# Two evictions of a gated attention and state-space kernel, written in another order of elements

## The chip, the core and the metric

The kernel runs on one core of one Trainium2 chip. The metric is the device time of one execution in microseconds. Before the change the median of three runs is 440.37 us (440.08 to 440.7). Busy times, waits and durations below come from one profiled execution, which took 440.81 us.

## The reference

The output mixes two branches of the same input `x` (2048 rows of 640 columns) by a gate computed for each row.

```
g = sigmoid((x * gate_w).sum(-1))
a = attention(x)      # 32 heads of 20; each row attends to 8 rows at a step of 2; then @ wo
b = conv(x)           # y = irfft(rfft(x) * rfft(K)) + x * Dskip, along the 2048 rows, for each column
K[d, l] = Re( sum_n C[d,n] * exp(dt[d] * A[d,n] * l) * dt[d] * B[d,n] )    # 640 columns, 192 states
out = g * a + (1 - g) * b
```

The change lies in branch `b`, where the kernel makes the generated filter `K` (its states are summed over n) and its spectrum.

## The kernel before

Two branches run interleaved on one core. The attention branch projects q, k and v (line 276, TensorE), multiplies q by shifted k (line 334, VectorE), sums over heads, takes the softmax, weighs v (line 403, VectorE), gathers (line 409) and projects with wo (line 426), and stores its gated result to DRAM as `gaS`.

The convolution branch has these stages:

- **Generation of K** (`KGen.plan`). For each of 10 blocks of 8 columns, TensorE forms arguments (line 758, tile `ar`), ScalarE takes sines and exponentials of them (lines 770 and 772, tile `big`), VectorE multiplies these (lines 789 to 791, tile `tbx`), and TensorE sums over the states (line 807, tile `kps`, one buffer of 320 fp32 values per partition). The task `fin` (line 864) evicts `kps` to the tile `E` in SBUF as bf16. There are 20 such evictions, two for each block.
- **Rearrangement** (`KSpec.half`): `E` goes through TensorE (line 881) to the tile `KE` (line 885).
- **Spectrum of K** (`KSpec.spectrum`): for 16 pairs of frequencies and for the real and the imaginary part, TensorE multiplies `KE` by weights `W` that SP streams from DRAM (lines 901 and 912; 20 matmuls each, and 4 more with `KD` for the real part). A real part is put in tile `ar` (two buffers, shared with other stages), an imaginary part in tile `kp` (one buffer); each is 2 banks x 320 fp32 values per partition. The task `ske` (line 916) evicts it to `sk`, which is the tile `bufA`, as bf16. There are 32 such evictions, 25 on ScalarE and 7 on VectorE.
- **Spectrum of x** (`Conv.first`, line 1022, tile `big`; `Conv.spectra`, line 1055, tile `ar`, evicted to `tbx` by line 1062), and the product of both spectra on VectorE (lines 1074 to 1080), which reads `sk` and writes its result back into `sk`.
- **Inverse** (line 1104, tile `cy`, evicted to `C` by line 1112) and **tail** (lines 1146 to 1173).

Both tasks of the change call the helper `evict`, so the profile shows them under line 457 (ScalarE) or 459 (VectorE): `E<-kps` is `fin`, and `bufA<-ar` and `bufA<-kp` with 128x640 elements are `ske`. (`bufA<-ar` with 128x1024 elements is the transposed input, another task.)

The order of all work is a list of task numbers written out by hand, `SEQ` (lines 50 to 88); a letter behind a number names the engine. `Plan.emit` issues the tasks in that order, and every engine runs its own instructions strictly in it. Tiles with a limited number of buffers make a producer wait until the consumer of an older buffer is done.

The layouts that matter, in elements of a partition: `E` is [20 m][2 h][2 a][40 x], so one step in m is 160 elements (320 bytes) and eight x of one `fin` lie together. `sk` is [2 r][320 x][32 f], so one step in x is 32 elements (64 bytes), and the two f of one `ske` lie together. In `kps` the order is [8 q][2 a][20 m]; in `ar` and `kp` it is [2 f][4 g][80 x] with f in two banks, 2048 bytes apart.

Of the kernel before, what the change touches and what calls it, by code (L numbers as in the profile page):

```python
# [450 lines left out]
def queue(nc, e):  # L451
    return {"S": nc.sync, "G": nc.gpsimd, "A": nc.scalar}[e]


def evict(nc, en, o, i):
    if en == "A":
        nc.scalar.activation(o, i, ACT.Identity)  # L457
    else:
        nc.vector.tensor_copy(o, i)  # L459
# [7 lines left out]
CQ = 8  # L467
# [4 lines left out]
NM = len(MS)  # L472
# [353 lines left out]
class KSpec:  # L826
# [32 lines left out]
    def fin(self, pl, c, h, b, m, m0, fins):  # L859
        nc = self.nc  # L860
        cl = c % NHF

        def fn(en):
            evict(nc, en, self.E[:, :, h, :, CQ * cl:CQ * cl + CQ].rearrange("p m a q -> p q a m"), b["kps"][:, 0:2 * NM * CQ].rearrange("p (q a m) -> p q a m", a=2, m=NM))
        return pl.add(f"fin{c}{h}", "AD", fn, deps=[m] + (self.moved if c == NHF and not h else []), after=fins[-1:], rel=[("kb", m0)])

    def half(self, pl, p, fs, pa, ident):
# [22 lines left out]
    def spectrum(self, pl, ps, sk, opened, free, ends):  # L890
        nc = self.nc
        out, prev, ld = {}, None, None
        for k in range(32):
            i, ro = divmod(k, 2)
            w, b = {}, {}

            def load(e, k=k, w=w):
                opened()
                w["t"] = self.W[self.nW % 4]
                self.nW += 1  # L900
                queue(nc, e).dma_start(w["t"][:].rearrange("p f m x -> p (f m x)"), self.w_d[k])
            ld = pl.add(f"wl{k}", "S", load, deps=self.past, after=[ld], acq=["W"])

            def spec(_, ro=ro, w=w, b=b):
                kp = b["kp"] = ps[ro]().tile([128, 2, 512], F32, name=("ar", "kp")[ro])
                first = -1 if ro == 0 else 0
                for m in range(first, M5):
                    for fl in range(2):
                        for c in range(2):
                            wt = self.one[:] if m < 0 else w["t"][:, fl, m, :]  # L910
                            ke = self.KD[:, c] if m < 0 else self.KE[:, m, c]
                            nc.tensor.matmul(kp[64 * c:64 * c + 64, fl, 0:320], wt, ke.rearrange("p g x -> p (g x)"),  # L912
                                             start=(m == first), stop=(m == M5 - 1), skip_group_check=True, tile_position=(0, 64 * c))

            def ev(en, i=i, ro=ro, b=b):
                evict(nc, en, sk[:, ro, :, 2 * i:2 * i + 2].rearrange("p (x g) f -> p f g x", g=4), b["kp"][:, :, 0:320].rearrange("p f (g x) -> p f g x", g=4))
            tag = ("ar", "kp")[ro]
            m = pl.add(f"ks{ro}x{i}", "P", spec, deps=[ld, self.kd] + self.kevs + (ends if ro else []), after=[prev], acq=[tag], rel=[("W", ld)])
            prev = m
            out[i, ro] = pl.add(f"ske{ro}x{i}", "AD", ev, deps=[m] + free, rel=[(tag, m)])  # L920
        return out
# [390 lines left out]
```

## Time and profile before

| | us |
|---|---|
| median of 3 runs | 440.37 |
| profiled execution | 440.81 |
| its span, first to last instruction | 439.0 |
| ScalarE (ACT) busy | 353.6 |
| VectorE (DVE) busy | 336.0 |
| TensorE (PE) busy | 326.6 |
| GpSimd (POOL) busy | 51.2 |

The stages in the span: projections and parameters up to about 90 us; generation of K beside attention from 88 to 275 us; the spectrum of K from 278 to 405 us, first beside line 1022 and the rest of attention, then beside line 1055 and the products; the inverse from 406.6 us; the stores at the end. The rows give an engine, a line, the operation, output and input tile, the form of each, the count, the busy time and the mean duration of one, and behind the bar the idle time of that engine just before these instructions with what ended it.

### The profile page before, as it was taken

How to read it: one execution, taken by the hardware profiler on the slowest of the kernel's cores; microseconds unless marked ns; L12 is line 12 of the kernel's file. 1: busy time of each engine (PE TensorE's matmuls, PEld its weight loads, DVE VectorE, ACT ScalarE, POOL GpSimd, SP SyncE). 2: the span in 40 equal slices, each digit the busy share in tenths (PEclk: the TensorE clock that was granted, in tenths of full speed). 3: DMA queues.
4: the chain of work that ended last, by engine and by line, in shares of the span. 5: the costliest groups of instructions: out<-in, count | busy, mean ns of one | idle time of the engine just before them, and what ended most of it. 6: DMA issues, size and time to landing. Idle time of an engine off the chain costs nothing. (4 is left out here: it accounts for less than half of the span.)

```text
span 439.0 us, 10744 instructions
## 1 busy us (share of the span) xinstructions
PE 326.6 (74%) x4553; PEld 216.3 (49%) x4574; DVE 336.0 (77%) x414; ACT 353.6 (81%) x424; POOL 51.2 (12%) x89
## 2 busy tenths in 40 slices
PE   0198998946889879888797899896876655763870
PEld 0164554422444444454244577784755545652850
DVE  5869998829998989998878996788575644932973
ACT  2499888955799999999999988743889988489892
POOL 5020182400003000005001010000030000000013
PEclk9999999975799999999769999999899997889796
DMA  8831366851025402607956061511167211180027
GB/s 294 309 89 45 104 183 134 167 114 37 19 66 112 105 18 60 137 14 142 155 115 140 20 132 47 127 51 45 46 158 228 60 37 41 46 198 1 3 52 190
DMA packets 50297, 44.34 MB, mean 101 GB/s; under 512 B 28890, under 2 KB 44794, under 8 KB 49994
## 3 DMA queue, kind: packets, MB, share of 16 engines
q1 hardware_dynamic: 44458, 24.90, 24.1%
q0 software_dynamic: 4784, 17.94, 15.7%
q10 hardware_dynamic: 1008, 0.82, 0.6%
q8 instruction: 35, 0.57, 0.6%
q14 instruction: 12, 0.10, 0.1%
HBM read 31.76 MB, written 11.89 MB: 99 GB/s over the span
## 5 line engine op out<-in xcount | busy, mean ns | idle before, releaser
L770 ACT ACTIVATE big<-ar 128x576 bf16<-128x576 int16 x120 | 72.6, 672 | 15.2 <-PE ar L758 14.0
L276 PE MATMUL tb<-bufA 128*128 128x512 bf16 x279 | 70.1, 384 | 5.5 <-issue 1.6
L758 PE MATMUL ar<-Rarg,L 64*128 64x288 bf16 (+1 forms) x480 | 55.6, 286 | 18.6 <-ACT big L772 8.8
L457 ACT ACTIVATE bufA<-ar 128x640 bf16<-128x640 f32 (+1 forms) x23 | 53.5, 2355 | 9.2 <-PE ar L184 5.6
L403 DVE TENSOR_TENSOR pv<-vc,asb 128x4096 bf16<-128x4096 bf16 (+1 forms) x24 | 46.0, 1928 | 13.2 <-DMA asb<-aS 8.7
L912 PEld LDWEIGHTS <-W 128*64 128x64 bf16 x640 | 47.1, 120 | 11.4 <-issue 8.5
L772 ACT ACTIVATE big<-ar 128x832 bf16<-128x832 f32 x60 | 49.6, 904 | 0.9 <-PE ar L758 0.5
L276 PEld LDWEIGHTS <-bufA 128*128 128x128 bf16 x300 | 33.5, 119 | 32.6 <-issue 9.3
L758 PEld LDWEIGHTS <-L 64*128 64x128 bf16 x480 | 21.5, 95 | 55.0 <-issue 49.7
L457 ACT ACTIVATE bufA<-kp 128x640 bf16<-128x640 f32 x11 | 34.9, 3173 | 8.0 <-PE kp L912 8.0
L807 PE MATMUL kps<-tbx 64*64 64x40 bf16 (+1 forms) x1280 | 28.5, 189 | 9.8 <-DVE E L459 8.6
L912 PE MATMUL kp<-KE,W 128*64 128x320 bf16 x320 | 28.8, 330 | 7.5 <-ACT bufA L457 5.7
L807 PEld LDWEIGHTS <-tbx 64*64 64x64 bf16 (+1 forms) x1280 | 25.2, 115 | 17.6 <-issue 14.9
L1055 PE MATMUL ar<-big,L 128*64 128x320 bf16 x128 | 14.9, 317 | 23.2 <-ACT bufA L457 17.5
L426 PE MATMUL tb<-wo_sb,oT 128*128 128x320 bf16 x160 | 27.2, 311 | 2.6 <-DVE ga L437 2.5
L912 PE MATMUL ar<-KE,W 128*64 128x320 bf16 x320 | 27.1, 318 | 0.0
L334 DVE TENSOR_TENSOR prod<-qk 128x2048 bf16<-128x2048 bf16 x20 | 24.1, 1228 | 3.5 <-PE lg L340 2.1
L1074 DVE TENSOR_TENSOR E<-tbx,bufA 128x1280 bf16<-128x1280 bf16 (+1 forms) x22 | 13.9, 656 | 16.6 <-ACT bufA L457 16.6
L457 ACT ACTIVATE big<-ar 128x1024 bf16<-128x1024 f32 x18 | 18.7, 1065 | 9.1 <-PE ar L1022 9.1
L459 DVE CAST tbx<-ar 128x640 bf16<-128x640 f32 x13 | 10.6, 821 | 19.5 <-PE ar L1055 19.4
L457 ACT ACTIVATE E<-kps 128x320 bf16<-128x320 f32 x15 | 24.1, 1609 | 0.6 <-PE kps L807 0.6
L791 DVE TENSOR_TENSOR tbx<-big 128x1280 bf16<-128x1280 bf16 x30 | 24.4, 815 | 0.0
(166 smaller groups left out, 620.7 us busy)
## 6 DMA issues: line engine op xcount, KB each, us to landing
W<-c_spec SPq DMA_DIRECT2D x32, 160.0 KB, 2.2
vc<-vS POOLq DMA_DIRECT2D x10, 327.5 KB, 7.1
Sprm<-pc SPq DMA_DIRECT2D x12, 240.0 KB, 3.0
L<-Sprm SPq DMA_DIRECT2D x80, 36.0 KB, 2.0
gaS<-ga SPq DMA_DIRECT2D x16, 160.0 KB, 2.9
uga<-in_A_x_dram POOLq DMA_DIRECT2D x8, 320.0 KB, 8.5
asb<-aS SPq DMA_DIRECT2D x16, 128.0 KB, 2.9
vc<-vS SPq DMA_DIRECT2D x6, 327.5 KB, 5.2
```

What stands on the lines that cost most here:

```text
L276: nc.tensor.matmul(ppf[:], self.wq[:, kt, which * D + e:(which + 1) * D:5], self.xT[:, c0 // 1024, kt, c0 % 1024:c0 % 1024 + SC], start=(k ...
L334: nc.vector.tensor_tensor(b[e][:], self.part(ch, 0)[:, e, o:o + C].unsqueeze(1).to_broadcast([128, W, C]), win(self.part(ch, 1)[:, e, :], ...
L403: nc.vector.tensor_tensor(b["pv", e][:, 0:2 * n], taps, aw, ALU.mult)
L426: nc.tensor.matmul(apf[:, :320], b["oT"][:, e, i * 128:(i + 1) * 128], wo_sb[:, e, hf * 320:(hf + 1) * 320], start=(e == 0), stop=(e == 4))
L457: nc.scalar.activation(o, i, ACT.Identity)
L758: nc.tensor.matmul(ar[:, g2, a0:a0 + ncol], L[rows, sb, gp, l0:l0 + 128], R[rows, c0:c0 + ncol], start=True, stop=True, tile_position=(64 ...
L770: nc.scalar.activation(dst[:, 2 * gp:2 * gp + 2, sub], ar[:].bitcast(I16)[:, :, 0:2 * SW:2].rearrange("p g (q n) -> p g q n", q=4), ACT.Si ...
L772: nc.scalar.activation(dst[:, 2 * gp:2 * gp + 2].rearrange("p g s q n -> p g (s q) n"), ar[:, :, 0:2 * EW].rearrange("p g (q n) -> p g q n ...
L791: nc.vector.tensor_tensor(qq[:, :, :, :], trg[:, :, KI:].rearrange("p a (v m) -> p a v m", v=2), exq[:, :, KI:].unsqueeze(2).to_broadcast( ...
L807: nc.tensor.matmul(kps[64 * w:64 * w + 64, 2 * NM * ql:2 * NM * ql + 2 * NM], pt[rows, v, k:k + 2, :].rearrange("p a n -> p (a n)"), qq[ro ...
L912: nc.tensor.matmul(kp[64 * c:64 * c + 64, fl, 0:320], wt, ke.rearrange("p g x -> p (g x)"), start=(m == first), stop=(m == M5 - 1), skip_g ...
L1055: nc.tensor.matmul(fp[64 * c2:64 * c2 + 64, fl, 0:320].rearrange("p (c x) -> p c x", x=32), self.phi(kg.hold, fb)[:, 2 * hf + fl, r, :], s ...
```

## The change

Both evictions go through the same elements, read from and written to the same addresses, in another order of loops.

```diff
@@ KSpec.fin
-            evict(nc, en, self.E[:, :, h, :, CQ * cl:CQ * cl + CQ].rearrange("p m a q -> p q a m"), b["kps"][:, 0:2 * NM * CQ].rearrange("p (q a m) -> p q a m", a=2, m=NM))
+            evict(nc, en, self.E[:, :, h, :, CQ * cl:CQ * cl + CQ], b["kps"][:, 0:2 * NM * CQ].rearrange("p (q a m) -> p m a q", a=2, m=NM))
@@ KSpec.spectrum
-                evict(nc, en, sk[:, ro, :, 2 * i:2 * i + 2].rearrange("p (x g) f -> p f g x", g=4), b["kp"][:, :, 0:320].rearrange("p f (g x) -> p f g x", g=4))
+                evict(nc, en, sk[:, ro, :, 2 * i:2 * i + 2].rearrange("p (x g) f -> p x g f", g=4), b["kp"][:, :, 0:320].rearrange("p f (g x) -> p x g f", g=4))
```

`fin` before: the innermost loop runs over m, so it reads neighbouring fp32 values of PSUM and writes each bf16 value 320 bytes behind the last. After: the innermost loop runs over q, so it reads at steps of 160 bytes and writes runs of eight neighbouring values (16 bytes).

`ske` before: the innermost loop runs over x, so it reads neighbouring values and writes at steps of 256 bytes (4 x 64). After: the innermost loop runs over f, so it reads in turn from two banks, and writes pairs of neighbouring values (4 bytes), with 64 bytes from pair to pair.

The list `SEQ` is word for word the same in both kernels. On TensorE, GpSimd and SP all rows of the program are the same; on ScalarE and VectorE the same instructions stand in the same places, and only the forms of these two evictions differ. Two places show it. On ScalarE, in the last part of the generation of K (`oT` is attention's, `big` the spectrum of x):

```order
 L435 ACTIVATE ga<-tb,g_sb 128x320
 L457 ACTIVATE oT<-tb 128x512
-L457 ACTIVATE E<-kps 128x8x2x20
+L457 ACTIVATE E<-kps 128x20x2x8
 L457 ACTIVATE big<-ar 128x1024 x2
 L770 ACTIVATE big<-ar 128x2x4x72
```

Nothing moves; eight q, two a and twenty m have become twenty m, two a and eight q. On VectorE, where the first spectra of K are evicted beside the end of attention:

```order
 L459 CAST oT<-tb 128x512
 L403 TENSOR_TENSOR pv<-vc,asb 128x4096
-L459 CAST bufA<-kp 128x2x4x80
-L459 CAST bufA<-ar 128x2x4x80
+L459 CAST bufA<-kp 128x320x2
+L459 CAST bufA<-ar 128x320x2
 L459 CAST oT<-tb 128x256
 L403 TENSOR_TENSOR pv<-vc,asb 128x4096
 L459 CAST big<-ar 128x1024
```

Again only the form differs: the output is now 320 places with two neighbouring values each.

## The prediction

> **What bounds the kernel now.** I read the busy shares first, then a table by stage, then the evictions by shape, then TensorE's waits in the stage where most of them lie.
>
> ```profile
> span 439.0 us, 10744 instructions
> PE 326.6 (74%) x4553; PEld 216.3 (49%) x4574; DVE 336.0 (77%) x414; ACT 353.6 (81%) x424; POOL 51.2 (12%) x89
> ```
>
> No engine is full over the whole span, so the stages must be looked at one by one. The table by stage has the stretch, its length, then the busy time of PE, PE's weight loads, DVE, ACT and POOL, then the granted TensorE clock:
>
> ```profile
> 125.00:275.00 150.00, 131.40 (x2046) 76.59 (x2054) 132.20 (x164) 142.87 (x205) 14.77 (x23) 0.95 0.43 90
> 190.00:275.00 85.00, 73.97 (x1200) 45.28 (x1200) 72.04 (x87) 79.87 (x113) 9.68 (x13) 0.92 0.49 98
> 275.00:300.00 25.00, 20.16 (x303) 18.09 (x301) 20.92 (x14) 12.45 (x12) 0.00 (x0) 1.00 0.32 78
> 300.00:407.00 107.00, 69.69 (x800) 58.14 (x801) 60.95 (x74) 84.68 (x47) 3.63 (x7) 0.91 0.33 88
> ```
>
> From 125 to 275 us ScalarE is busy for 142.9 of 150 us: it sets the pace of the generation of K. From 300 to 407 us nobody is full: ScalarE 79%, TensorE 65%, VectorE 57%. There the engines wait for each other in turn. The evictions, by duration in ns (least, median, most):
>
> ```profile
> L457 ACT ACTIVATE bufA<-kp x11: 3014/3077/3398, 310.6 to 401.6; 128x640 bf16<-128x640 f32 x11
> L457 ACT ACTIVATE E<-kps x15: 1560/1603/1663, 126.0 to 271.1; 128x320 bf16<-128x320 f32 x15
> L459 DVE CAST bufA<-kp x5: 2987/3007/3124, 286.4 to 372.8; 128x640 bf16<-128x640 f32 x5
> L459 DVE CAST E<-kps x5: 1534/1556/1568, 100.2 to 189.1; 128x320 bf16<-128x320 f32 x5
> ...
> L457 ACT ACTIVATE tbx<-ar x19: 698/705/1062, 303.1 to 404.4; 128x640 bf16<-128x640 f32 x19
> L457 ACT ACTIVATE C<-cy x13: 1018/1023/1045, 407.8 to 419.7; 128x1024 bf16<-128x1024 f32 x13
> L459 DVE CAST tbx<-ar x13: 806/824/826, 300.3 to 400.6; 128x640 bf16<-128x640 f32 x13
> L459 DVE CAST C<-cy x7: 1214/1214/1223, 412.0 to 419.7; 128x1024 bf16<-128x1024 f32 x7
> ```
>
> The reader is to see that `bufA<-kp` and `tbx<-ar` have the same 640 elements, types and memories, yet take 3014 and 705 ns. Only the order of addresses differs. From 705 ns for 640 and 1023 ns for 1024 elements, ScalarE takes 318/384 = 0.83 ns an element and 175 ns besides; VectorE in the same way 390/384 = 1.02 ns and 174 ns. The slow evictions take (3014-175)/640 = 4.4 ns an element on ScalarE and (2987-174)/640 = 4.4 ns on VectorE, and `E<-kps` (1560-175)/320 = 4.3 ns. Two engines of different speed arrive at one price, so the price belongs to the isolated 2-byte write, not to the engine.
>
> Rows in order of time show what it does to the stage, PE first, then ACT:
>
> ```profile
> 343.98 0.46 PE L912 MATMUL ar<-KD,one 128*64 128x320 bf16 x4 [1.18 <-ACT bufA L457]
> 346.87 1.55 PE L912 MATMUL kp<-KE,W 128*64 128x320 bf16 x20 [1.07 <-ACT bufA L457]
> 349.73 0.46 PE L912 MATMUL ar<-KD,one 128*64 128x320 bf16 x4 [1.31 <-ACT bufA L457]
> ...
> 343.42 3.40 ACT L457 ACTIVATE bufA<-kp 128x640 bf16<-128x640 f32 x1
> 346.32 3.36 ACT L457 ACTIVATE bufA<-ar 128x640 bf16<-128x640 f32 x1
> 349.18 3.37 ACT L457 ACTIVATE bufA<-kp 128x640 bf16<-128x640 f32 x1
> ```
>
> Evictions stand back to back on ScalarE, one each 2.9 us, and TensorE stops before nearly every group until a buffer is free.
>
> **The change part by part.** No instruction, wait or transfer is added, removed or moved; 52 evictions get another duration, and what follows is the effect of that.
>
> *Price of `fin`.* It will write runs of 16 bytes. The nearest rows write 8 bytes and hop: `C<-cy` above (160-byte hops, 0.83 ns an element), and line 1079, whose output is `bufA` in runs of 8 bytes with 64 bytes from run to run, beside line 1077, whose output is contiguous:
>
> ```profile
> L1079 DVE TENSOR_TENSOR bufA<-E,tbx 128x1280 bf16<-128x1280 bf16 x7 | 6.0, 855 | 0.2
> L1077 DVE TENSOR_TENSOR tbx<-tbx,bufA 128x1280 bf16<-128x1280 bf16 x7 | 5.8, 825 | 0.2
> L435 ACT ACTIVATE ga<-tb,g_sb 128x320 bf16<-128x320 f32 x20 | 10.6, 543 | 6.9 <-PE tb L426 5.2 <-issue 1.6
> L437 DVE TENSOR_SCALAR ga<-tb,g_sb 128x320 bf16<-128x320 f32 x12 | 6.6, 556 | 4.5 <-PE tb L426 3.8 <-issue 0.6
> ```
>
> 855 against 825 ns: hops between 8-byte runs cost next to nothing. So `fin` falls to what 320 elements cost, 0.54 us on ScalarE and 0.56 on VectorE (`ga`). Saved: 15 x 1.07 = 16 us of ScalarE, 5 x 1.0 = 5 us of VectorE.
>
> *Price of `ske`.* Nothing in the trace writes 4-byte pairs 64 bytes apart. Bounds: `tbx<-ar` writes 4-byte pairs 8 bytes apart and reads in turn from two banks, as `ske` will; that gives 0.70 us. If a pair costs what an isolated value costs now, it is 320 x 4.4 + 175 = 1.58 us. I take 0.75 us on ScalarE and 0.85 on VectorE, near the row that also reads from two banks and also writes pairs. Saved: 25 x 2.3 = 57 us of ScalarE and 7 x 2.2 = 15 us of VectorE; with the upper bound 1.4 us each.
>
> *From 300 to 407 us.* TensorE's waits there, grouped by what came after:
>
> ```profile
> L912 PE MATMUL kp<-KE,W 128*64 128x320 bf16 x280 | 25.6, 334 | 7.5 <-ACT bufA L457 5.7 <-DVE bufA L459 1.7
> L1055 PE MATMUL ar<-big,L 128*64 128x320 bf16 x120 | 14.1, 318 | 23.1 <-ACT bufA L457 17.5 <-DVE bufA L459 2.7 <-ACT tbx L457 2.1
> L912 PE MATMUL ar<-KD,one 128*64 128x320 bf16 x56 | 7.2, 328 | 2.7 <-ACT bufA L457 2.5
> L426 PE MATMUL tb<-wo_sb,oT 128*128 128x320 bf16 x30 | 4.6, 299 | 2.5 <-DVE ga L437 2.5
> L1104 PE MATMUL cy<-GAB,bufA 64*128 64x128 bf16 x10 | 0.7, 306 | 4.0 <-DVE bufA L1079 4.0
> ```
>
> Waits ended by a `ske`: 5.7 + 1.7 + 17.5 + 2.7 + 2.5 = 30.1 us. Most are 1.1 to 1.4 us long as in the rows of time, less than the 2.3 us that one eviction gives back, and the longest stand behind two:
>
> ```profile
> 365.90 6.20 ACT L457 ACTIVATE bufA<-ar 128x640 bf16<-128x640 f32 x2
> ...
> 401.56 3.36 ACT L457 ACTIVATE bufA<-kp 128x640 bf16<-128x640 f32 x1
> 404.40 1.04 ACT L457 ACTIVATE tbx<-ar 128x640 bf16<-128x640 f32 x1
> ```
>
> Two queued evictions shrink from 6.2 to 1.5 us. I let all 30.1 us go. The 2.5 us on `ga` go too, since VectorE had a 3.0 us `ske` ahead of it; of the waits on `tbx` 1.5 of 2.1; of the 4.0 us before the inverse 1.7, because the last eviction, `tbx` at 404.40 us and the products come earlier but remain a chain. The clock: 69.7 us of TensorE at 0.91 would be some 63.5 at 1.00, which the stage ahead of it has; the cold stretches follow the long waits, and I count 4.5 us. Sum 30.1 + 2.5 + 1.5 + 1.7 + 4.5 = 40.3 us.
>
> Then other things are late: runs of line 1055 that wait for `tbx`, and VectorE's products (52 us of work after its four `ske` here shrink) standing ahead of casts in its queue. I charge 8 us (between 0 and 18), leaving **32 us**. A second way agrees: 64 us of TensorE at the share that it has from 190 to 275 us, where all three engines are busy (74.0/85 = 87%), makes 73.5 us, 33 less than 107.
>
> *From 275 to 300 us.* Three `ske` on VectorE and one on ScalarE hold TensorE up; its waits on them go, **2.3 us**:
>
> ```profile
> L1022 PE MATMUL ar<-F1c,uga 128*64 128x128 bf16 x172 | 11.1, 273 | 2.3 <-ACT bufA L457 1.4 <-DVE bufA L459 0.9
> ```
>
> *From 100 to 275 us.* All 15 `fin` of ScalarE lie from 125 to 275 us. They take 16 of its 142.9 us, leaving 127; but VectorE has 132 - 2 and TensorE 131. If they now ran at ScalarE's old share, 95%, the stage would take 138 us, 12 less; if half of ScalarE's 16 us came through, 8. I take **9 us** (3 to 15). Ahead of it TensorE once waits 8.6 us for a `fin` on VectorE, which comes late for a DMA and only ends 1.0 us sooner: **1 us**.
>
> ```profile
> L807 PE MATMUL kps<-tbx 64*64 64x40 bf16 x96 | 2.4, 195 | 8.6 <-DVE E L459 8.6
> ```
>
> *Sum.* 32.3 + 2.3 + 9 + 1 = 44.6 us off the profiled 440.81 us (span 439.0 and 1.8 around it): 396.2 us. The median of the runs is 0.4 us lower: **396 us**. Before 100 us and from the inverse on nothing changes.
>
> **Rivals.**
>
> *The pair costs a full hop.* `ske` takes 1.58 us. For it speaks that one price holds for both engines, which looks like a price for each place written; against it that 8-byte runs are free. TensorE's short waits still go, long ones only in part: 24 instead of 30.1 us, less on `ga`, and 10 us of new waits, so 23 in that stage, 2 before it, 10 for `fin`: 406 us. [...]
>
> *The fixed order gives the time back.* Waits on `tbx` and on VectorE's products replace the old ones (18 instead of 8 us in the stage), and generation gains 3 instead of 9, because VectorE, 88% busy there, takes ScalarE's place: 32.3 - 10 + 3 + 2.3 + 1 = 28.6 us off, 412 us. For it speaks that no engine's queue is rearranged; against it that every engine's own work in the stage, at most 64 us, is far below 107.
>
> *Slower: reading PSUM at steps costs more than the writes give.* If each of the 640 reads, now never a neighbour of the last, cost 4.4 ns as isolated writes do, and the hops of pairs 1.4 us besides, `ske` would take 4.4 us: 1.4 us more for each of the 24 on ScalarE after 300 us, some 34 us, about 474 us. It decides once a `ske` is over 3.0 us. The read price alone would give 2.99 us, and 1.58 for `fin`: no change, 440 us. Against both: `tbx<-ar` reads in turn from two banks and `C<-cy` at steps of 512 bytes, both at 0.83 ns. [...]
>
> **How the numbers follow.** Forecast 0.63 (384 to 404), the pair's hop 0.18 (400 to 410), the order 0.14 (406 to 425), slower 0.03, no change 0.02. The low end of the range takes no new waits (8 off), 15 for generation (6 off): 382; the high end, 412, holds the hop and half of the order's cases. About 0.2% is what a measurement of this kernel can tell from no change. Faster 0.95, same 0.02, slower 0.03.
>
> **What would show it.** In the new profile `E<-kps` near 0.5 us and `bufA<-kp` near 0.75 us; over 1.4 us is the first rival. TensorE's waits ended by `bufA` near zero and the stage from the last `E<-kps` to line 1104 some 33 us shorter; if `tbx` or lines 1074 to 1080 end its waits instead, it is the second. ScalarE's busy time should fall to about 280 us. The prediction fails if ScalarE's fall is there and the inverse still starts after 380 us.

## The result, and the profile after

The changed kernel takes 380.39 us (median of 4 runs, 376.92 to 381.9), beside 440.23 us for the kernel before in the same session (438.53 to 440.7). The ratio is 0.8636, with a 95% interval of 0.8571 to 0.8701: 59.8 us less. The forecast was 396 us, 44.6 less, with a range from 382 to 412. The direction and the mechanism held; the time fell 1.6 us below the range, because several terms of the sum were too small. The intervals of the series here reach 0.5 to 0.8% to each side, not the 0.2% that the prediction had taken.

The page's first lines, span and busy time of each engine:

```profile
span 379.3 us, 10744 instructions
PE 312.1 (82%) x4553; PEld 202.8 (53%) x4574; DVE 315.2 (83%) x414; ACT 282.3 (74%) x424; POOL 52.7 (14%) x89
```

ScalarE fell from 353.6 to 282.3 us (forecast: about 280). Now no engine stands out: VectorE and TensorE are at 83% and 82%. The four evictions by duration (least, median, most in ns; first and last start):

```profile
L457 ACT ACTIVATE E<-kps x15: 431/450/557, 123.8 to 253.6; 128x320 bf16<-128x320 f32 x15
L457 ACT ACTIVATE bufA<-kp x11: 702/727/751, 284.1 to 343.9; 128x640 bf16<-128x640 f32 x11
...
L459 DVE CAST E<-kps x5: 483/485/491, 98.8 to 181.6; 128x320 bf16<-128x320 f32 x5
L459 DVE CAST bufA<-kp x5: 816/819/825, 266.6 to 330.6; 128x640 bf16<-128x640 f32 x5
```

A `ske` takes 727 and 819 ns, from 3077 and 3007; a `fin` 450 and 485 ns, from 1603 and 1556. What ended TensorE's waits from 265 to 375 us (total, times, longest):

```profile
PE ar L912 <- DMA W<-c_spec: 4.5, 1, 4.5
PE cy L1104 <- DVE bufA L1079: 2.5, 1, 2.5
...
PE tb L426 <- ACT ga L435: 1.6, 1, 1.6
...
PE ar L1055 <- DVE tbx L459: 0.7, 1, 0.7
PE ar L1055 <- ACT tbx L457: 0.6, 1, 0.6
PE kp L912 <- DMA W<-c_spec: 0.3, 1, 0.3
```

No wait is ended by a `ske` any more (`bufA` from line 457 or 459); those were 30.1 us from 300 us on. The longest wait is a new one, 4.5 us for the weights `W`. Before, TensorE never waited for `W` in this stage.

Stretch by stretch, from the first starts of lines in both traces (us):

| from, to | before | after | change | forecast |
|---|---|---|---|---|
| start, first `pv` (L403) | 96.0 | 94.6 | -1.4 | 0 |
| to the first `fin` on ScalarE | 30.0 | 29.2 | -0.7 | -1 |
| to the last `fin` on ScalarE | 145.1 | 129.8 | -15.3 | -9 |
| to the first matmul of L1055 | 25.7 | 22.0 | -3.7 | -2.3 |
| to the inverse (L1104) | 109.8 | 71.3 | -38.5 | -32.3 |
| to the end | 32.4 | 32.4 | 0 | 0 |

### The profile page after: what moved, and what is told of

The parts are those of the page before. It is cut to its first block, busy times and chain, and to the rows that moved or that the text cites. A ratio compares the mean times of both kernels' runs of the same rounds, so it can differ in the third digit from the quotient of the medians.

```text
span 379.3 us, 10744 instructions
## 1 busy us (share of the span) xinstructions
PE 312.1 (82%) x4553; PEld 202.8 (53%) x4574; DVE 315.2 (83%) x414; ACT 282.3 (74%) x424; POOL 52.7 (14%) x89
## 4 chain that ended last, share of the span: by engine, by line
PE 39%; ACT 19%; DVE 17%; DMA 16%; issue 3%; SPq 3%; POOL 0%; POOLq 0%; DVEq 0%; ACTq 0%
PE ar L912 7%; PE kp L912 5%; ACT big L770 5%; PE ar L1022 5%; PE tb L276 4%; DMA ident<-c_ident 4%; ACT big L772 4%; PE ar L758 4%; PE tb L426 4%; PE kps L807 3%; DMA aS<-at 3%; PE tb L409 3%; DMA W<-c_spec 3%; DMA vc<-vS 3%; DMA asb<-aS 2%
## 5 line engine op out<-in xcount | busy, mean ns | idle before, releaser
L770 ACT ACTIVATE big<-ar 128x576 bf16<-128x576 int16 x120 | 71.0, 657 | 13.7 <-PE ar L758 12.6
L403 DVE TENSOR_TENSOR pv<-vc,asb 128x4096 bf16<-128x4096 bf16 (+1 forms) x24 | 46.0, 1929 | 8.8 <-DMA asb<-aS 7.7
L912 PEld LDWEIGHTS <-W 128*64 128x64 bf16 x640 | 40.1, 114 | 10.8 <-DMA W<-c_spec 5.5
L457 ACT ACTIVATE bufA<-ar 128x640 bf16<-128x640 f32 (+1 forms) x23 | 19.2, 842 | 20.0 <-PE ar L912 14.5
L912 PE MATMUL ar<-KE,W 128*64 128x320 bf16 x320 | 25.9, 310 | 4.5 <-DMA W<-c_spec 4.5
L912 PE MATMUL kp<-KE,W 128*64 128x320 bf16 x320 | 25.9, 310 | 0.3 <-DMA W<-c_spec 0.3
L457 ACT ACTIVATE tbx<-ar 128x640 bf16<-128x640 f32 x19 | 13.2, 701 | 15.1 <-PE ar L1055 8.3
L334 DVE TENSOR_TENSOR prod<-uga 128x2048 bf16<-128x2048 bf16 x20 | 24.1, 1221 | 0.1
L184 PE MATMUL ar<-ident,uga 128*128 128x128 bf16 x80 | 7.6, 262 | 19.8 <-DMA ident<-c_ident 19.4
L409 PE MATMUL tb<-pv,ind 128*64 128x512 bf16 (+1 forms) x192 | 21.5, 347 | 0.1
L789 DVE TENSOR_TENSOR tbx<-big 128x1024 bf16<-128x1024 bf16 x30 | 20.5, 685 | 0.9 <-ACT big L772 0.5
```

The lines of the kernel that those rows point to most:

```text
L334: nc.vector.tensor_tensor(b[e][:], self.part(ch, 0)[:, e, o:o + C].unsqueeze(1).to_broadcast([128, W, C]), win(self.part(ch, 1)[:, e, :], ...
L403: nc.vector.tensor_tensor(b["pv", e][:, 0:2 * n], taps, aw, ALU.mult)
L409: nc.tensor.matmul(b["op", e][64 * a:64 * a + 64, 0:n, :], self.twin, b["pv", e][:, a:2 * n:2, w, :], start=(w == 0), stop=(w == HV - 1), ...
L770: nc.scalar.activation(dst[:, 2 * gp:2 * gp + 2, sub], ar[:].bitcast(I16)[:, :, 0:2 * SW:2].rearrange("p g (q n) -> p g q n", q=4), ACT.Si ...
```

## The experiments

### Each half of the change alone

`fin` alone leaves line 916 as it was; `ske` alone leaves line 864 as it was.

Line 916 of `fin` alone:

```diff
-                evict(nc, en, sk[...].rearrange("p (x g) f -> p x g f", g=4), b["kp"][...].rearrange("p f (g x) -> p x g f", g=4))
+                evict(nc, en, sk[...].rearrange("p (x g) f -> p f g x", g=4), b["kp"][...].rearrange("p f (g x) -> p f g x", g=4))
```

> Only the eviction of kps to E has the new order; the 32 evictions of the spectrum are as before. Theory: the two edits act in two stages that do not touch each other, and ScalarE's time in the generation of K comes back in full. From 125 to 272 us some 15 us go and about 1 us ahead of it: 440.2 - 16 = 424 us (421 to 427), with E<-kps at 0.45 us and bufA<-kp still at 3.0. Rival: only part of it is fin's (the 9 us of the forecast), the rest came from the spectrum's edit or from chance between two profiles: 430 us or more.

> Only the evictions of the spectrum to bufA have the new order; the evictions of kps are as before. Theory: the stage from 278 us to the inverse gives back 3 + 38.5 us by itself: 440.2 - 42 = 398 us (395 to 401), and with the run of the other edit alone the two gains add up to the whole 60 us. Rival: the gains help each other (less pressure on memory, another clock), so that each alone gives less and they add up to 50 us or less: 404 us or more.

`fin` alone: 425.2 us (424.43 to 427.52), ratio 0.9677 [0.9629, 0.9725], 14.6 us off the 439.79 us of the kernel before beside it. `ske` alone: 396.95 us (395.14 to 398.98), ratio 0.9039 [0.898, 0.9099], 42.8 us off. Both lie where the theory had put them. Together they bring 57.4 us; both edits at once brought 59.8. So the two gains lie in different stages and add up, within intervals of 2 to 3 us each, and neither replaces the other's wait. With `ske` alone the stretch from line 1055 to the inverse is 69.0 us (292.1 to 361.1), from 109.8: the spectrum's gain is all its own.

### Which engine's `fin` carries the gain of the generation

The first kernel has the new order on ScalarE ("A"), the second, with "D" in its place, on VectorE.

```diff
-            evict(nc, en, self.E[...], b["kps"][...].rearrange("p (q a m) -> p m a q", a=2, m=NM))
+            if en == "A":
+                evict(nc, en, self.E[...], b["kps"][...].rearrange("p (q a m) -> p m a q", a=2, m=NM))
+            else:
+                evict(nc, en, self.E[...].rearrange("p m a q -> p q a m"), b["kps"][...].rearrange("p (q a m) -> p q a m", a=2, m=NM))
```

> The changed kernel in which the 5 evictions of kps on VectorE keep the old order (1.55 us each); the 15 on ScalarE have the new one (0.45 us). Theory: ScalarE set the pace of the generation of K, so nearly all of that stage's 15 us come from its 15 evictions; VectorE's are worth some 2 us: 382 to 384 us. Rival: VectorE's five, which TensorE once waited 8.6 us for, carry a good part: 387 us or more.

> The reverse: only the 5 evictions of kps on VectorE have the new order, the 15 on ScalarE the old one (1.6 us). Theory: the stage keeps ScalarE's pace, some 13 to 14 us are lost against the changed kernel: 393 to 396 us. Rival: 388 us or less, where VectorE's five carry a good part.

New order for ScalarE's 15 `fin` only: 382.92 us, ratio 0.8685 [0.8629, 0.8741]. For VectorE's 5 only: 395.45 us, ratio 0.8985 [0.892, 0.905]. The changed kernel beside them took 379.05 us, so ScalarE's 15 are worth 16.4 us and VectorE's five 3.9 us, each beside the new order on the other engine; both times are the expected ones. The 3.9 us are little more than the noise between the two series (about 3 us). The traces are sharper: from the first to the last `fin` on ScalarE the kernel with ScalarE's new order takes 130.3 us and the one with VectorE's 145.2 us, beside 145.1 before and 129.8 after the change. So all of that stage's gain comes with ScalarE's 15. They lose 15 x 1.15 = 17.3 us of work: nearly all of it reaches the end.

### How much of a `ske` still matters

```diff
-                evict(nc, en, sk[...], b["kp"][...])
+                for _ in range(2):
+                    evict(nc, en, sk[...], b["kp"][...])
```

> The changed kernel with each eviction of the spectrum done twice over, so that an eviction costs 1.4 to 1.6 us: the price of the first rival of the prediction, set by hand. 18 us of ScalarE and 6 us of VectorE are added. Theory: TensorE sets the pace there and a buffer of ar or kp is taken again only some 1.6 to 1.9 us later, so that little shows: 383 to 389 us. Rival one: evictions stand on the path, and all of ScalarE's 18 us show: 398 us. The prediction's own working for this price, 10 us over the forecast, would give 390 us.

388.74 us (387.83 to 390.77), ratio 0.8846 [0.88, 0.8891]: 8.3 to 9.7 us more than the changed kernel, for 17 us more on ScalarE (299.2 against 282.3) and 6 on VectorE. That is at the top of what the theory expected, and the rival's 398 us fell. Two `ske` in a row take some 1.45 us, and that kernel keeps 51 us of the gain, so that a `ske` at my upper bound of 1.58 us would have kept about 50 of the 60 us (an estimate). A few short waits for it return (lines behind 916 are one number further in this kernel):

```profile
PE ar L1056 <- ACT bufA L457: 2.8, 3, 1.4
```

The price of a `ske` below 1.5 us was the smaller half of the question; leaving 3 us was the larger.

### What the price belongs to: write step, pair or read step

The 16 pairs of frequencies take four orders in turn.

```diff
-                evict(nc, en, sk[...].rearrange("p (x g) f -> p x g f", g=4), b["kp"][...].rearrange("p f (g x) -> p x g f", g=4))
+                o = ("p x g f", "p g x f", "p f x g", "p f g x")[i % 4]
+                evict(nc, en, sk[...].rearrange("p (x g) f -> " + o, g=4), b["kp"][...].rearrange("p f (g x) -> " + o, g=4))
```

> The changed kernel in which the evictions of the spectrum take turns by pair of frequencies, in four orders: (0) the changed one, pairs 64 bytes apart; (1) pairs 256 bytes apart; (2) single values 64 bytes apart, read from PSUM at steps of 320 bytes; (3) the old one, single values 256 bytes apart, read as neighbours. Theory: the price is for a 2-byte value written without a neighbour, whatever the step: 0.7 us for 0 and 1, 3.0 us for 2 and 3 on ScalarE, 0.82 and 3.0 on VectorE. Rival one: the step of 256 bytes is the bad thing: 0 and 2 at 0.7 to 1.0 us, 1 at 1.5 us or more. Rival two: reads at steps cost too: 2 over 3.0 us, clearly slower than 3. The whole kernel, with half of the evictions slow, 395 to 412 us.

Rows in order of time of the kernel with four orders, ScalarE and then VectorE (start, duration, and in brackets the idle time before). The names don't show the order of loops; it follows from the place in the program: pairs 64 bytes apart (at 262.05), lone values 64 bytes apart with reads at steps of 320 bytes (281.35 and 286.58), pairs 256 bytes apart (303.60 and 304.96), lone values 256 bytes apart with neighbouring reads, as before the change (316.32). On VectorE the rows are pairs 64 bytes apart (266.90), pairs 256 bytes apart (275.08), lone values 256 bytes apart (297.07) and lone values 64 bytes apart (313.86):

```profile
262.05 0.71 ACT L457 ACTIVATE bufA<-ar 128x640 bf16<-128x640 f32 x1 [0.61 <-PE ar L912]
...
281.35 3.05 ACT L457 ACTIVATE bufA<-ar 128x640 bf16<-128x640 f32 x1 [0.93 <-PE ar L912]
286.58 3.00 ACT L457 ACTIVATE bufA<-kp 128x640 bf16<-128x640 f32 x1 [0.33 <-PE kp L912]
...
303.60 0.75 ACT L457 ACTIVATE bufA<-ar 128x640 bf16<-128x640 f32 x1 [1.18 <-PE ar L912]
304.96 0.73 ACT L457 ACTIVATE bufA<-kp 128x640 bf16<-128x640 f32 x1
...
316.32 3.09 ACT L457 ACTIVATE bufA<-ar 128x640 bf16<-128x640 f32 x1 [1.18 <-PE ar L912]
```

```profile
266.90 0.83 DVE L459 CAST bufA<-kp 128x640 bf16<-128x640 f32 x1
275.08 0.81 DVE L459 CAST bufA<-kp 128x640 bf16<-128x640 f32 x1
297.07 3.00 DVE L459 CAST bufA<-kp 128x640 bf16<-128x640 f32 x1
313.86 2.99 DVE L459 CAST bufA<-kp 128x640 bf16<-128x640 f32 x1 [4.62 <-PE kp L912]
```

On ScalarE pairs take 0.71 to 0.75 us at either distance, lone values 3.00 to 3.09 us at either distance; on VectorE 0.81 to 0.83 and 2.99 to 3.00 us. Lone values with strided reads cost no more than lone values with neighbouring reads (3.00 and 3.05 against 3.09), so the read step adds nothing to a lone write; what a step of 320 bytes would cost beside a fast write, these rows don't show. It is the lone 2-byte write that costs: (3.0 - 0.175) / 640 = 4.4 ns each, on both engines. This settles the first rival and the slower one at the instruction itself. The kernel as a whole, with half of its `ske` slow, took 401.6 us in its only run.

### The changed kernel once more, and a miss

> The changed kernel once more, as the measure for the three others of this call: 380 us (377 to 382).

379.05 us (378.53 to 381.86, 7 runs), ratio 0.8601 [0.8554, 0.8649]. A third series, with more about it below:

> The changed kernel once more on the same chip, as the measure for the run beside it: 380 us (377 to 382).

379.48 us (378.61 to 381.68), ratio 0.8609 [0.8562, 0.8656].

To see whether seven loads for the tail cause the new wait for `W`, I first tried to start them later, by more conditions on their tasks:

```diff
-            self.pse.append(pl.add(f"psi{k}", "SG", psi, deps=self.freed, after=self.pse[-1:]))
+            self.pse.append(pl.add(f"psi{k}", "SG", psi, deps=self.freed + [self.muls[(2, 4, 5, 5)[k], 0]], after=self.pse[-1:]))
```

> The changed kernel in which the 2.8 MB that GpSimd loads for the tail (psi, and gaS back into uga) are no longer all started from 295 to 299 us, but one after the other behind the products of later blocks of frequencies; added waits on GpSimd and SP, nothing else. Theory: the changed kernel's new wait of 4.5 us for W at 304 to 309 us, and the low clock behind it (two groups at 2.9 instead of 1.5 us), come from these loads filling the DMA engines: 7 us less than the changed kernel, 372 to 376 us. Rival one: W is late because SP issues it late or because only four buffers hold it, whatever else is loaded: 379 to 382 us. Rival two: the loads come too late for the tail: 383 us or more.

379.31 us (377.87 to 382.5), ratio 0.8615. This tells nothing on the question: such conditions are not waits on the chip, and the order is a list written out by hand, so the program came out the same as the changed kernel's: in its trace GpSimd starts the seven loads from 294.1 us on, all within 4 us, as ever. It counts as one more measurement of that, and its wait for `W` was 3.5 us.

### Where the new wait for `W` comes from

In the changed kernel's trace, GpSimd's queue in order of time, then TensorE's, then the stretch from 296 to 310 us (length, busy times, clock, DMA share, GB/s):

```profile
295.32 0.52 POOL L1126 DMA_DIRECT2D uga<-gaS  x1 [56.41 <-DMA gaS<-ga]
296.26 0.58 POOL L1120 DMA_DIRECT2D psi<-c_psi  x1 [0.42 <-ACT tbx L457]
296.83 1.47 POOL L1126 DMA_DIRECT2D uga<-gaS  x3
298.30 1.09 POOL L1120 DMA_DIRECT2D psi<-c_psi  x2
```

```profile
303.83 0.44 PE L912 MATMUL ar<-KD,one 128*64 128x320 bf16 x4
308.81 2.88 PE L912 MATMUL ar<-KE,W 128*64 128x320 bf16 x20 [4.54 <-DMA W<-c_spec]
311.48 2.88 PE L912 MATMUL kp<-KE,W 128*64 128x320 bf16 x20
314.15 0.59 PE L1055 MATMUL ar<-big,L 128*64 128x320 bf16 x4
314.57 0.44 PE L912 MATMUL ar<-KD,one 128*64 128x320 bf16 x4
314.84 1.52 PE L912 MATMUL ar<-KE,W 128*64 128x320 bf16 x20
```

```profile
296.00:310.00 14.00, 9.16 (x126) 7.02 (x122) 9.04 (x12) 4.95 (x8) 3.13 (x6) 0.91 0.98 259
...
308.00:314.00 6.00, 5.19 (x40) 3.59 (x42) 0.82 (x1) 0.70 (x1) 0.00 (x0) 0.50 0.55 195
```

GpSimd starts seven loads within 4 us, 2.8 MB that only the tail reads, from 361 us on. For 14 us the DMA engines are 98% busy, and `W` arrives late: the five loads of it that are issued there take 10.3 us to land (median), where the median of all 32 is 2.2. TensorE stands for 4.5 us, then runs at half the granted clock (0.50) for two groups, 2.88 us each in place of 1.52.

These loads stood at the same place before the change, from 323 us on. GpSimd's first and last rows there, and the 14 us from 323:

```profile
323.08 0.52 POOL L1126 DMA_DIRECT2D uga<-gaS  x1 [69.15 <-DMA gaS<-ga]
326.04 1.09 POOL L1120 DMA_DIRECT2D psi<-c_psi  x2
323.00:337.00 14.00, 9.46 (x120) 7.95 (x120) 8.70 (x11) 14.00 (x7) 3.63 (x7) 1.00 0.94 258
```

The DMA engines moved as much (258 GB/s), the four loads of `W` that were issued there took 7.8 us to land, and TensorE did not wait for them. What differs most is its pace: a group of 20 matmuls, which takes one load of `W`, started each 2.9 us then (321.04 to 335.48 us, five groups) and each 1.7 us now (293.29 to 300.08 us, four groups). So it takes the burst and the new pace together to make TensorE wait.

To test this, the seven loads go to SP's queue, spread between the loads of `W` (a task's number with S is SP's, with G GpSimd's):

```diff
-... 1213 546 1339G 1064 1067 1070
+... 1213 546 1064 1067 1070 1339S
-... 1222 1076 1077 1078A 1079 1082 1085 1088 1080 1083
+... 1222 1076 1335S 1077 1078A 1079 1082 1340S 1085 1088 1337S 1080 1083
-... 1094 1097 1100 1103
+... 1094 1341S 1097 1100 1103 1338S
```

(The last of the seven follows 1112. Further down the list, the other six entries with G go, here and in the two kernels after this one.)

> The run before that was to delay the tail's loads delayed nothing: the waits that it names are read by the planner alone and no engine sees them, so it was the changed kernel again. Now the seven loads themselves stand elsewhere: four of gaS (320 KB each) and three of psi (512 KB) move from GpSimd's queue, where all start within 4 us at 295 us, into SP's queue between the loads of W, one behind every second or third of these from the fifteenth on. Theory: these loads fill the DMA engines and hold W up; spread out, TensorE's 4.5 to 5.1 us wait for W goes and with it the two slow groups behind it: 371 to 375 us. Rival one: W is late for its four buffers or for SP's order: the wait stays, 378 us or more. Rival two: W queues behind the big loads on SP and waits more often: over 380 us.

374.4 us (372.85 to 374.75, 6 runs), ratio 0.8476 [0.8431, 0.8522], beside 379.48 us of the changed kernel on the same chip. This is the expected 371 to 375. The same stage in its trace, up to the inverse at 340.1 us, and what is left of the wait:

```profile
275.70:340.10 64.40, 58.27 (x799) 49.43 (x798) 52.09 (x73) 31.43 (x47) 0.00 (x0) 1.00 0.54 146
```

```profile
PE kp L912 <- DMA W<-c_spec: 0.9, 1, 0.9
```

The wait shrank from 4.5 and 0.3 to 0.9 us, and the clock is 1.00 throughout: TensorE's busy time is 58.3 us, which is what 61.3 us at 0.95 come to.

This kernel changed two things, the queue and the spreading. Two more part them. In the first, all seven go to SP's queue in one go, behind the same load of `W` where the spread ones began:

```diff
-... 1064 1067 1070
+... 1064 1067 1070 1339S 1335S 1340S 1337S 1341S 1338S 1345S
```

In the second, all seven stand behind the last load of `W`:

```diff
-... 1271 1272 1273 1335G 1336S 1340G 1341G
+... 1271 1272 1273 1339S 1335S 1340S 1336S 1341S 1337S 1345S 1338S
```

> The changed kernel with the seven loads for the tail on SP's queue, as in the kernel with spread loads (374.4 us), but all seven behind one load of W, one after another. It parts two causes of the wait for W: the burst, or GpSimd's queue. Theory (burst): 2.8 MB ahead of the next W, at the 259 GB/s that the changed kernel moved from 296 to 310 us, are some 11 us; three W stand ready and last about 3.3 us each, so TensorE waits 1 to 5 us for W again, the granted clock drops behind it, and the time is 376 to 381 us. Rival (GpSimd's queue is what delays W, and SP's queue serves them at the pace of need): no wait for W over 1 us, 373 to 375 us.

> The changed kernel with the seven loads on SP's queue behind the last load of W, at about 331 us, so none of them stands beside the spectrum of K. Theory: no wait for W at all; 4.1 MB (these seven and five that stood there already) land within some 12 us, by 345 us, ahead of the tail that starts at 354 us; the time is 372 to 375 us, like the spread loads or a little better. Rival: the tail's data come too late, TensorE waits for psi or the last products for uga, and the time is 376 to 382 us.

In one go: 384.48 us (383.46 to 385.92), ratio 0.8705 [0.8639, 0.8772], slower even than the changed kernel. The rival fell; the theory's kind held, but the time lies above its 376 to 381 us, and the wait was twice what I had worked out:

```profile
303.84 1.52 PE L912 MATMUL ar<-KE,W 128*64 128x320 bf16 x20
314.73 2.88 PE L912 MATMUL kp<-KE,W 128*64 128x320 bf16 x20 [9.36 <-DMA W<-c_spec]
```

Without GpSimd's queue the wait is there and longer, so the burst is enough and GpSimd's queue is not needed. (Here `W` stands behind the burst in one queue, in the changed kernel beside it in another; a burst spread out on GpSimd's own queue was not run.) Two things in my working were wrong. The burst began at 299.0 us, the first `W` behind it was issued at 302.8 us, and its group started at 314.7, 15.7 us after the burst began, where I had counted 11. And the cover, TensorE's work on loads that are there already, was too long: I had counted 3.3 us of it for each load of `W`, but there are 32 loads for 32 groups of 20 matmuls, so a load lasts for one group and what stands beside it, some 1.75 us (in the kernel below, SP issues 20 of them in 34.9 us).

Behind the last `W`: 374.19 us (373.06 to 375.44), ratio 0.8461 [0.8386, 0.8537]. There is no wait for `W` at all, and the inverse starts at 338.3 us, 1.8 us earlier than with spread loads. But the whole is no better, because the inverse and the tail now stand still for the following (3.8 us; in the other kernels 0 to 1.1 us):

```profile
PE cy L1104 <- issue: 2.2, 2, 1.1
PE cy L1146 <- issue: 1.6, 2, 0.8
```

From 330 to 345 us the DMA engines are 100% busy in this kernel, at 239 GB/s, which makes 3.6 MB; these twelve loads are 4.6 MB (4 of 512 and 8 of 320 KB), not the 4.1 of the expectation, and do not land by 345 us. That the burst there causes these pauses too is likely by its time, but not shown. Both kernels with moved loads beat the changed one by 5 us, 1.3%.

## Why the prediction was right in kind and too small

**Prices: right.** `ske` 0.73 and 0.82 us (forecast 0.75 and 0.85), `fin` 0.45 and 0.485 (0.54 and 0.56). The conclusion "the price belongs to the isolated 2-byte write" is now shown, on both engines. For the pair, the slowest of the changed kernel's `bufA<-kp` took 0.751 us on ScalarE and 0.825 on VectorE, far below the upper bound of 1.58.

**Before the first changed instruction: -1.4 us that are scatter.** The first `pv` waits for a DMA and started 1.4 us earlier in this one execution (94.6 against 96.0 us). Line 403 stands ahead of every `fin`, so it is not the change's. In the traces of before, after, each half alone and `ske` twice, which are alike up to that point, it starts at 96.0, 94.6, 95.9, 94.5 and 93.9 us; why that transfer's time varies is open.

**100 to 125 us: right.** The stall behind VectorE's `fin` ends 1.06 us sooner after `pv`; 0.3 of that was lost again up to ScalarE's first `fin`.

**Generation: the term that was mis-sized first, 9 us forecast, 15.3 measured.** The stage from the first to the last `fin`, of before and of after (length, then busy time of PE, its weight loads, DVE, ACT and POOL, clock):

```profile
125.70:272.50 146.80, 128.58 (x2005) 74.65 (x2015) 129.00 (x161) 140.22 (x201) 14.77 (x23) 0.95 0.44 91
```

```profile
123.50:255.00 131.50, 125.29 (x2023) 72.40 (x2033) 125.87 (x161) 124.27 (x201) 16.14 (x23) 0.97 0.49 102
```

The failed step was "if half of ScalarE's 16 us came through, 8", which had no row behind it, together with a ceiling that was too high. Of ScalarE's 16 us (140.2 to 124.3) 15.3 came through, nearly twice that half. I had set VectorE at 130 and TensorE at 131 us from a window that ran on to 275 us, 2.5 us past the stage: in the stage itself they had 129.0 and 128.6. Then VectorE lost 3.1 us, and TensorE 3.3, of which the clock (0.95 to 0.97) makes 2.6. At ScalarE's old share, 95%, VectorE's 125.9 us come to 132.5; the stage took 131.5. So three engines at 95% could share a stage after all (95.3, 95.7 and 94.5%). Which of them sets its end now is not shown. VectorE alone it hardly is: where it kept the old order, two slow `fin` gave it 1.5 us more work between ScalarE's first and last `fin` (126.2 us against 124.6 to 124.7), and the stretch took 130.3 us, within the 129.8 to 130.4 of three traces of the changed kernel. That ScalarE set the pace before is shown by the two half kernels: 130.3 us with its 15 `fin` in the new order, 145.2 with VectorE's five.

**The stage up to the inverse: 32.3 forecast, 38.5 measured.** The same stretch by its TensorE rows:

```profile
296.80:406.60 109.80, 70.01 (x800) 58.23 (x801) 63.75 (x74) 84.68 (x47) 3.63 (x7) 0.91 0.32 86
```

```profile
275.60:347.00 71.40, 61.32 (x803) 50.83 (x804) 52.38 (x74) 31.37 (x47) 3.65 (x7) 0.95 0.50 131
```

TensorE's idle time falls from 39.8 to 10.1 us (29.7 less) and its busy time from 70.0 to 61.3 (8.7 less). By the terms of the forecast:

| term | forecast | measured |
|---|---|---|
| waits ended by `ske` | 30.1 | 30.1 |
| `ga` | 2.5 | 0.9 |
| `tbx` and the end | 3.2 | 2.9 |
| clock | 4.5 | 3.2 |
| new waits | -8 | -4.8 |
| not in the sum | 0 | 6.1 |
| sum | 32.3 | 38.4 |

The clock is 70.0 x 0.09 - 61.3 x 0.05 = 3.2. The charge for new waits was too large, and of the wrong kind: I had named `tbx` and VectorE's products, and what came is `W`, 4.5 + 0.3 us, beside loads that stood there before as well and did no harm at TensorE's old pace. That wait also costs most of the clock that is still missing, as the kernel with spread loads shows (64.4 us for the stage).

The larger part of the 6.1 us outside the sum is something I had not read rightly in the rows of before. There a group of 20 matmuls that is followed by a wait counts 1.55 us of busy time (the group at 346.87 in the prediction's rows, then 1.31 us of idle, then the next at 349.73: 2.86 us from start to start). After the change the same group is followed at once:

```profile
300.08 1.52 PE L912 MATMUL ar<-KE,W 128*64 128x320 bf16 x20
301.44 0.44 PE L1055 MATMUL ar<-big,L 128*64 128x320 bf16 x4
```

1.36 us from start to start, with the two busy times overlapping. So such a wait cost 1.50 us, not the 1.31 shown: the last matmul's end counts as busy, and work that follows at once would have covered it. TensorE pauses 24 times in this stage before and 6 times after; if each hides as much, that is an estimate of 18 x 0.19 = 3.4 us. The idle total differs from the named waits by 0.6, and some 2.1 us I cannot place.

**275 to 300 us:** 3.7 us in place of 2.3, in the same direction; the waits on `ske` are gone there as well.

**From the inverse on nothing changes: right,** 32.4 us in both.

**The rivals.** A pair at a full hop fell by the 0.73 us. "The fixed order gives the time back" fell in its size: it is there, as a wait for `W`, and takes 5 us with the clock it costs (379.48 against 374.4 us; 7.0 us of this stage between the two profiled executions), not 10 us beyond my charge. "Slower by strided reads" fell by the four orders. As for the range, its low end allowed no new waits and 15 us for the generation, but nothing for waits that cost more than they show, and nothing for a stray 1.4 us ahead of the change. Two later series of the changed kernel (379.05 and 379.48 us) lie below it too.

## What to carry to other kernels

Compare evictions of one size on one engine before anything else: here equal elements at 4.4 times the time (3077 against 705 ns) came from the order of addresses, and it was enough to let two neighbouring bf16 values be written one after the other (727 ns). When a stage gets faster, look again at the transfers beside it: here seven loads that cost no wait where TensorE took a `W` each 2.9 us made it wait 4.5 us where it took one each 1.7 us. Issue those with slack behind the ones that are waited for; here the seven in one go took back 5 us. And a wait can cost more than the trace shows: a wait of 1.31 us cost 1.50 here, by what the engine's last instruction would have overlapped.

## What the runs showed of the hardware

- A lone 2-byte write to SBUF cost 4.4 ns on ScalarE and VectorE alike at steps of 64 and 256 bytes (4.3 at 320); with two neighbouring ones at either of the first two steps, 640 elements took 0.71 to 0.75 us on ScalarE and 0.81 to 0.83 on VectorE, near the 0.705 and 0.824 of `tbx<-ar`.
- `bufA<-kp` after the change, which reads fp32 from PSUM in turn from two banks, took 0.70 to 0.75 us for 640 elements on ScalarE, 0.82 to 0.90 ns an element beside the prediction's 175 ns; `uga<-tb`, which reads neighbours, took 0.597 us for 512, 0.82 ns. Reads at steps of 320 bytes added nothing to the price of lone writes (3.00 and 3.05 us against 3.09).
- After 4.5 us without a matmul the granted clock was at half (0.50) for the next 5.4 us, so that this wait cost about 7 (two groups of 2.88 in place of 1.52 us); after 9.4 us one group took 2.88 us.
- 2.8 MB of loads in one go held up a 160 KB load that TensorE needed, from GpSimd's queue (4.5 us) and from the same queue (9.4 us), where TensorE took one such load each 1.7 us; where it took one each 2.9 us, the same loads cost no wait.
